# Seven half products of an expert layer in another order, and the weight sums of the first token tile made sooner

## The chip, the cores and the metric

One core of a Trainium2 chip runs the whole program. The metric is device time in microseconds (us); the core is the only one, so its time is the time. Before the change three runs gave 745.58, 746.56 and 749.73 us.

## The reference, cut to what matters

Attention with a sigmoid in place of the softmax, then a layer with three projections and a maximum, then a mixture of experts in which each token goes to one expert:

```python
for e in range(E):                       # E = 8, 1792 tokens, D = 768, F = 1024
    mask = e_idx == e
    h = np.maximum(x[mask] @ w1[e], 0.0)
    out[mask] = gate_w[mask, None] * (h @ w2[e])
```

The change lies in `h @ w2[e]`. All inputs are fp32.

## The kernel before, in words

**Token tiles.** Tokens are sorted by expert into static tiles. The first three (tile 0, 1, 2; 512, 512 and 448 tokens) take the route described here; the fourth (384 tokens, `last`) multiplies by `w2` directly, and a loop takes more tiles if there are any. Each tile has its own expert, whose weights are loaded for it: `raw[1]` (w1, three loads of 1 MB) and `raw[2]` (w2, four loads of 768 KB, one of them into the tile `rawb`).

**Precision by splitting.** Each fp32 operand is split into a rounded part and a rest (`split`, lines 183 to 189: an ACT copy, then a DVE subtraction), and each product is three matmuls: rounded by rounded, rounded by rest, rest by rounded. So every weight chunk costs ACT and DVE one instruction each (`ck_split`, line 828), and it is issued four steps ahead (`ahead`, line 1081) into a ring of six buffers.

**Steps of a tile.** n = 0 to 11: layer 1 (`mm1`, line 894), twelve chunks of 12 matmuls; four quarters q of the hidden rows, three chunks each. The results stand in PSUM banks named t, a0, a1, a0 for q = 0 to 3. n = 12 to 25: layer 2 by a scheme with seven half-size products in place of eight (Strassen's idea, in Winograd's form), two chunks of 12 matmuls (128x384) each (`mm2_prod`, line 920). The hidden half matrices are called A11, A12, A22, their sums S1 to S4, the weight quarters B11 to B22, their sums T1 to T4. The order in `PRODS` (line 825), with the bank and whether the product starts the bank or adds onto what is there:

- A11·B11 starts t; S2·T2 starts a1; A12·B21 adds onto t; S3·T3 adds onto a1; S1·T1 starts a0; A22·T4 starts t; S4·B22 adds onto a0.

I call them by these names. A product that adds onto a bank has to wait until the partial result in it was read (`read_prod`, line 933): ACT reads A11·B11 (lines 941, 942) and A12·B21 (line 944), DVE reads the others, two instructions each (line 948), scaled by the gate into four output rows `xo`. The read of product j is issued after the first chunk of product j+1.

**What else is queued on DVE in these steps.** `half_sums` (line 847) makes S1 to S4 and the splits of the A's from the banks of layer 1; four instructions of the last quarter, which read a0, are put off and issued one per step at n = 12 to 15 (`later`; lines 883 to 886, the last of them line 863 for A22). `split_sum` (line 888) splits S3, S1 and S4 in two halves, each into the buffer of a matrix that is done: S3 over A11, S1 over S2, S4 over A12. `make_sum` (line 821) makes the T's, two instructions each, in the place of B12 (T3), B11 (T1), B21 (T4) and in `tw` (T2 = T3 + B11); T1 and T4 subtract T2. `gather_T` (line 779) turns the next tile's tokens: transposes on PE after n = 19, 21 and 23, with an ACT copy and a DVE subtraction each.

**What sets the order.** PE, ACT, DVE and SP run in the order in which the program writes them; no scheduler moves anything. The main loop (line 1118) issues per step: the matmuls, `read_prod`, `split_sum` by the table `parts`, one of `later`, `gather_T`, the chunk splits four steps ahead, and `make_sum` by the table `make` (one table for tile 0, one for the others). In tile 0 the steps of layer 1 run in the order n = 0, 1, 3, 4, 6, 7, 2, 5, 8 to 11 (line 1076), and its four loads of `raw[2]` are held until the matmuls of the steps before positions 2, 3, 5 and 6 are done (line 1129).

```python
        make = [{9: "T3 0 T2 0", 10: "T3 1 T2 1", 12: "T1 0", 13: "T1 1"},
                {5: "T3 0", 6: "T2 0 T3 1", 7: "T2 1", 9: "T1 0", 10: "T1 1"}]
        parts = {2: ("S3", 0), 3: ("S3", 1), 5: ("S1", 0), 6: ("S1", 1), 9: ("S4", 0), 10: ("S4", 1)}
```

Of the kernel before, what the change touches and what calls it, by code (L numbers as in the profile page):

```python
# [16 lines left out]
ALU = mybir.AluOpType  # L17
# [11 lines left out]
def attn_moe_kernel(  # L29
# [15 lines left out]
    nc = tc.nc  # L45
# [37 lines left out]
    def cut(a, off, *shape):  # L83

        n = 1
        for s in shape:
            n *= s
        a = a[:, off:off + n]
        if len(shape) == 2:
            a = a.rearrange("p (a b) -> p a b", a=shape[0])  # L90
        elif len(shape) == 3:
            a = a.rearrange("p (a b c) -> p a b c", a=shape[0], b=shape[1])
        return a
# [89 lines left out]
    def split(dR, dL, src, alone=False):  # L183

        if alone:
            nc.vector.tensor_copy(out=r(dR), in_=src)
        else:
            nc.scalar.activation(out=r(dR), in_=src, func=ACTF.Copy)  # L188
        nc.vector.tensor_tensor(out=r(dL), in0=src, in1=dR, op=ALU.subtract)  # L189
# [183 lines left out]
    with tc.manual_schedule(engines={mybir.EngineType.PE, mybir.EngineType.Activation, mybir.EngineType.DVE, SP}):  # L373
# [84 lines left out]
        for e in range(E):  # L458
            nc.vector.scalar_tensor_tensor(out=bias_t[:, :, e], in0=midf, scalar=mb[:, 0, e:e + 1], in1=bias_t[:, :, e],
                                           op0=ALU.mult, op1=ALU.add)  # L460
# [346 lines left out]
        HC = DM // 2  # L807
# [3 lines left out]
        def quad(k, c):  # L811

            k = {"T1": "B11", "T3": "B12", "T4": "B21"}.get(k, k)
            if k == "T2":
                return tw[0][:, c]
            n = int(k[2]) - 1
            return raw[2][2 * int(k[1]) - 2 + c][:, :, HC * n:HC * (n + 1)]
# [3 lines left out]
        def make_sum(k, c):  # L821
            d, a, b = (quad(x, c) for x in (k,) + SUMS[k])
            nc.vector.tensor_tensor(out=d, in0=a, in1=b, op=ALU.add if k == "T2" else ALU.subtract)  # L823

        PRODS = (("A11", "B11", 0, True), ("S2", "T2", 1, True), ("A12", "B21", 0, False), ("S3", "T3", 1, False),
                 ("S1", "T1", 2, True), ("A22", "T4", 3, True), ("S4", "B22", 2, False))

        def ck_split(n, i=None):

# [2 lines left out]
            if n >= N1 and i is not None and i < NF:  # L832
                j, c = divmod(n - N1, 2)
                b = [cut(buf, DM * a, 2, HC) for a in range(2)]
                split(b[0], b[1], quad(PRODS[j][1], c))
                return b
# [11 lines left out]
        st = {}  # L848
# [71 lines left out]
        def mm2_prod(n, w):  # L920
            j, c = divmod(n - N1, 2)
            k, _, g, first = PRODS[j]
            if first and c == 0:
# [7 lines left out]
                                         stop=(c == 1 and f == 1 and m == 2), skip_group_check=not first)  # L931

        def read_prod(j, i, ix):
            o = st["g", PRODS[j][2]]
            for s in range(2):
                src = o[:, s, 0:HC]
                d0, d1 = xo[s], xo[2 + s]
                g0, g1 = (gcol[:, i % 2, 2 * h + s:2 * h + s + 1] for h in range(2))
                lo, hi = slice(0, HC), slice(HC, DM)
                if j == 0:  # L940
                    nc.scalar.activation(out=d0[:, hi], in_=src, func=ACTF.Copy, scale=g0)
                    nc.scalar.activation(out=d1[:, lo], in_=src, func=ACTF.Copy, scale=g1)
                elif j == 2:
                    nc.scalar.activation(out=d0[:, lo], in_=src, func=ACTF.Copy, scale=g0)
                else:
                    d, g, add = {1: (d0[:, hi], g0, d0[:, hi]), 3: (d1[:, lo], g1, d1[:, lo]), 4: (d1[:, hi], g1, d1[:, lo]),
                                 5: (d1[:, lo], g1, d1[:, lo]), 6: (d0[:, hi], g0, d0[:, hi])}[j]
                    nc.vector.scalar_tensor_tensor(out=d, in0=src, scalar=g, in1=add, op0=ALU.mult, op1=ALU.add)  # L948
                if j >= 5:
                    scatter(d1 if j == 5 else d0, ix[(2 if j == 5 else 0) + s])  # L950

# [17 lines left out]
        def scatter(d, ix):  # L969
            dm = nc.gpsimd.indirect_dma_start(out=out, out_offset=bass.IndirectOffsetOnAxis(ap=ix, axis=0),  # L970
                                              in_=d[:, 0:DM], in_offset=None, bounds_check=NT - 1, oob_is_err=False)
            if not tc.in_control_flow:
                for o_ in outs:
                    tc.declare_no_dep(dm.ins, o_, reason="each token is in one tile only")
                outs.append(dm.ins)
# [117 lines left out]
        for p in range(P0, TT):  # L1093
# [3 lines left out]
            else:  # L1097
# [12 lines left out]
        first = gather(ixs[0], (1,))  # L1110
        early = []
        steps = {N1 + 7: 0, N1 + 9: 1, N1 + 11: 2}
        make = [{9: "T3 0 T2 0", 10: "T3 1 T2 1", 12: "T1 0", 13: "T1 1"},
                {5: "T3 0", 6: "T2 0 T3 1", 7: "T2 1", 9: "T1 0", 10: "T1 1"}]
        for m in make:
            m.update({17: "T4 0", 18: "T4 1"})
        parts = {2: ("S3", 0), 3: ("S3", 1), 5: ("S1", 0), 6: ("S1", 1), 9: ("S4", 0), 10: ("S4", 1)}
        for p, (i, n) in enumerate(todo):
            last = i == NF
            nt = SH if last else MD if i == NF - 1 else GT  # L1120
# [8 lines left out]
            if i == 0 and p in (2, 3, 5, 6):  # L1129
                d = wl.popleft()()  # L1130
# [31 lines left out]
            if not last and n >= N1:  # L1162
                if n > N1 and (n - N1) % 2 == 0:
                    read_prod((n - N1) // 2 - 1, i, ixs[i])
                if n - N1 in parts:
                    split_sum(*parts[n - N1])
                if later:
                    later.popleft()()
                if n == NCW - 1:
                    read_prod(6, i, ixs[i])  # L1170
# [18 lines left out]
        d = xo[xo_n[0] % 4]  # L1189
        g = gcol[:, NF % 2, 2:3]  # L1190
# [65 lines left out]
```

## Time and profile before

| what | us |
|---|---|
| median of three runs (lowest, highest) | 746.56 (745.58, 749.73) |
| the profiled execution, its own time | 743.39 |
| its span, first to last instruction | 741.6 |
| seven products of tile 0, tile 1, tile 2, with the transposes among them | 39.2, 33.0, 33.4 |

The span is that of the one profiled execution; 1.8 us of its own time lie outside of it. A line of the profile names an engine, an operation and its source line, with the tiles it writes and reads: `oacc` are the banks of the seven products, `hacc` those of layer 1, `wo_ck` the ring of weight chunks, `hx` the split hidden matrices, `raw`, `rawb` and `tw` the weights and their sums.

### The profile page before, as it was taken

The page shows a single profiled execution, that of the slowest core. Times are in us where ns is not written, and L with a number is a line of the kernel's source. Part 1 is how long each engine was busy: PE and PEld are TensorE (multiplying, and loading weights), DVE is VectorE, ACT ScalarE, POOL GpSimd, SP SyncE. Part 2 cuts the span into 40 slices and gives each one's busy share as a digit, 9 for nine tenths or more (in the row PEclk, how much of TensorE's full clock was granted, in tenths as well). Part 3 has the DMA queues.
Part 4 walks back from the last instruction along what each step waited for, and adds up shares of the span by engine and source line. Part 5 has one row for each costly group of instructions (what it writes and reads, how often), then busy time and mean ns, then how long its engine had stood idle before and what let it go on. Part 6 is the DMA issues. An engine that isn't in the chain of part 4 may idle for free.

```text
span 741.6 us, 10670 instructions
## 1 busy us (share of the span) xinstructions
PE 726.5 (98%) x4164; PEld 615.7 (83%) x4164; DVE 486.7 (66%) x845; ACT 262.9 (35%) x410; POOL 70.4 (9%) x96
## 2 busy tenths in 40 slices
PE   9999999999999999999999999999799999999996
PEld 6455455799898989989899988988698899989996
DVE  4677784666977879684036574136983896699463
ACT  5675556001010010101025433333652373465252
POOL 3000000000000000000001007351023005000101
PEclk9999999999999999999999999999999999999999
DMA  8866670142431222300001116556063026315101
GB/s 204 210 163 162 184 203 32 44 128 85 149 108 65 85 86 63 130 0 1 1 0 45 58 51 200 175 198 269 4 219 120 1 86 230 137 40 183 57 2 62
DMA packets 42330, 78.58 MB, mean 106 GB/s; under 512 B 6201, under 2 KB 28794, under 8 KB 42276
## 3 DMA queue, kind: packets, MB, share of 16 engines
q1 hardware_dynamic: 38420, 66.10, 29.1%
q0 software_dynamic: 3776, 11.63, 4.6%
q8 instruction: 35, 0.57, 0.4%
q14 instruction: 19, 0.16, 0.1%
q10 hardware_dynamic: 80, 0.11, 0.0%
HBM read 69.79 MB, written 11.58 MB: 110 GB/s over the span
## 4 chain that ended last, share of the span: by engine, by line
PE 88%; DVE 7%; ACT 2%; issue 1%; POOL 0%; POOLq 0%; ACTq 0%; DVEq 0%
PE acc L499 35%; PE hacc L901 12%; PE X L344 8%; PE oacc L929 7%; PE s L318 7%; PE acc_b L563 5%; PE acc_a L563 4%; PE oacc L917 3%; PE acc_c L563 3%; DVE wo_ck L189 2%; PE X L352 1%; PE xT L788 1%; PE s L334 1%; DVE raw L823 1%; DVE hx L863 1%
## 5 line engine op out<-in xcount | busy, mean ns | idle before, releaser
L499 PE MATMUL acc<-xR,w_ring 128*128 128x512 f32 (+1 forms) x864 | 208.2, 362 | 0.0
L499 PEld LDWEIGHTS acc<-xR,w_ring 128*128 128x128 f32 x864 | 157.6, 188 | 17.7 <-issue 0.7
L901 PE MATMUL hacc<-xh,wo_ck 128*128 128x512 f32 (+3 forms) x600 | 121.9, 363 | 0.0
L901 PEld LDWEIGHTS hacc<-xh,wo_ck 128*128 128x128 f32 x600 | 107.2, 188 | 13.3 <-issue 0.3
L499 PE MATMUL acc<-xLa,w_ring 128*128 128x512 f32 (+1 forms) x360 | 101.3, 362 | 0.0
L929 PE MATMUL oacc<-wo_ck,hx 128*128 128x384 f32 x504 | 93.7, 341 | 7.2 <-DVE xo L948 5.4
L929 PEld LDWEIGHTS oacc<-wo_ck,hx 128*128 128x128 f32 x504 | 88.5, 191 | 9.5 <-issue 4.6
L301 ACT ACTIVATE at<-s,nlns 128x896 f32<-128x896 f32 x84 | 77.9, 1006 | 44.9 <-PE s L318 43.5
L189 DVE TENSOR_TENSOR wo_ck<-raw,wo_ck 128x512 fp32r<-128x512 f32 (+1 forms) x87 | 68.1, 805 | 24.2 <-ACT wo_ck L188 24.2
L499 PEld LDWEIGHTS acc<-xLa,w_ring 128*128 128x128 f32 x360 | 66.3, 188 | 7.1
L188 ACT ACTIVATE wo_ck<-raw 128x512 fp32r<-128x512 f32 (+1 forms) x87 | 59.6, 729 | 20.9 <-DVE raw L823 10.0
L318 PEld LDWEIGHTS s<-kq 64*128 64x128 f32 x432 | 38.1, 186 | 20.9 <-issue 15.5
L318 PE MATMUL s<-kq 64*128 64x448 f32 x432 | 51.3, 378 | 0.0
L503 ACT ACTIVATE hA<-acc 128x1024 f32<-128x1024 f32 (+1 forms) x8 | 7.4, 922 | 118.3 <-PE acc L499 118.3
L480 DVE SCALAR_TENSOR_TENSOR gk<-wof,gk 128x768 f32<-128x768 f32 x48 | 45.9, 956 | 1.4
L994 POOL MEMSET xo<- 128x544 f32 x5 | 2.6, 554 | 410.4 <-PE acc_a L563 381.8
L775 POOL DMA_INDIRECT xg<-x2d,idx x30 | 30.6, 1021 | 79.9 <-PE xT L788 50.1
L344 PE MATMUL X<-at,u 128*64 128x448 f32 x192 | 37.8, 543 | 0.0
L370 DVE CAST xR<-X 128x448 fp32r<-128x448 f32 x24 | 14.8, 619 | 32.1 <-PE X L352 32.1
L505 DVE TENSOR_TENSOR hB<-hB,acc 128x1024 f32<-128x1024 f32 (+1 forms) x8 | 8.7, 1087 | 39.5 <-PE acc L499 39.4
L188 ACT ACTIVATE w_ring<-cv 128x768 fp32r<-128x768 f32 x14 | 11.8, 842 | 54.7 <-PE acc L499 54.7
L505 DVE TENSOR_TENSOR hA<-hA,acc 128x1024 f32<-128x1024 f32 (+1 forms) x16 | 17.4, 1086 | 20.3 <-PE acc L499 19.9
(259 smaller groups left out, 885.5 us busy)
## 6 DMA issues: line engine op xcount, KB each, us to landing
stage<-in_moe_w_dram SPq DMA_DIRECT2D x18, 768.0 KB, 4.6
raw<-in_moe_w_dram SPq DMA_DIRECT2D x12, 1024.0 KB, 5.4
u<-in_qk_dram SPq DMA_DIRECT2D x46, 224.0 KB, 4.7
raw<-in_moe_w_dram SPq DMA_DIRECT2D x12, 768.0 KB, 5.6
stage<-in_moe_w_out_dram SPq DMA_DIRECT2D x6, 768.0 KB
x2d<-xo SPq DMA_DIRECT2D x28, 128.0 KB, 1.7
gk<-wgT SPq DMA_DIRECT2D x8, 384.0 KB, 5.5
rawb<-in_moe_w_dram SPq DMA_DIRECT2D x4, 768.0 KB, 5.9
```

What stands on the lines that cost most here:

```text
L188: nc.scalar.activation(out=r(dR), in_=src, func=ACTF.Copy)
L189: nc.vector.tensor_tensor(out=r(dL), in0=src, in1=dR, op=ALU.subtract)
L301: nc.scalar.activation(out=dst, in_=s[:, :, 0:S], func=ACTF.Sigmoid, scale=qscale, bias=nlns)
L318: nc.tensor.matmul(s[g][:, h, 0:S], r(kt[p, a, 0, 128 * g:128 * (g + 1)]), r(kt[p, x, 1]), start=(n == 0), stop=(n == 2))
L344: nc.tensor.matmul(X_t[u][64 * h:64 * h + 64, 0:S], vt[:, 2 * g + h], at[:, 2 * g + h], start=(g == 0), stop=False)
L480: nc.vector.scalar_tensor_tensor(out=junk, in0=wof[kb], scalar=1.0, in1=wgb[e % 2], op0=ALU.mult, op1=ALU.mult, accum_out=gw[:, kb, e:e + 1])
L499: nc.tensor.matmul(acc[:, c, 0:cw], r(m[:, a, kk, :]), r(x[kk][:, c0 + cw * c:c0 + cw * (c + 1)]), start=(kk == 0 and n == 0), stop=(kk == ...
L505: nc.vector.tensor_tensor(out=dst, in0=dst, in1=acc[:, :, 0:cw], op=ALU.max)
L563: nc.tensor.matmul(acc, r(hs[:, a, kk, :]), r(w(kk, b)), start=(kk == 0 and n == 0), stop=(kk == KB - 1 and n == 2))
L775: d = nc.gpsimd.indirect_dma_start(out=xg[s][:, XC[c][0]:XC[c][1]], out_offset=None, in_=x2d[c], in_offset=bass.IndirectOffsetOnAxis(ap=ix ...
L901: st["mm"] = nc.tensor.matmul(acc[:, f, t0:t1], r(w[a][:, k, 128 * f:128 * (f + 1)]), r(x[:, 2 * c + k, t0:t1]), start=(t0 == 0 and c == 0 ...
L929: nc.tensor.matmul(o[:, s, 0:HC], r(hz[k][:, x, 2 * c + f, 128 * s:128 * (s + 1)]), r(w[a][:, f]), start=(first and c == 0 and f == 0 and ...
```

## The change

The order of `PRODS`, of the split sums and of the reads is altered, and the sums of tile 0 get other steps. The new order is A11·B11, S2·T2, A12·B21, S1·T1, S3·T3, A22·T4, S4·B22. S1·T1 (fourth) is not read after it; with the read of S3·T3 (fifth), DVE issues four instructions: per 128 tokens one that reads a1 and one that reads a0 and adds what the first has written.

```diff
-        PRODS = (("A11", "B11", 0, True), ("S2", "T2", 1, True), ("A12", "B21", 0, False), ("S3", "T3", 1, False),
-                 ("S1", "T1", 2, True), ("A22", "T4", 3, True), ("S4", "B22", 2, False))
+        PRODS = (("A11", "B11", 0, True), ("S2", "T2", 1, True), ("A12", "B21", 0, False), ("S1", "T1", 2, True),
+                 ("S3", "T3", 1, False), ("A22", "T4", 3, True), ("S4", "B22", 2, False))
...
         def read_prod(j, i, ix):
+            if j == 3:
+                return
...
-                    d, g, add = {1: (d0[:, hi], g0, d0[:, hi]), 3: (d1[:, lo], g1, d1[:, lo]), 4: (d1[:, hi], g1, d1[:, lo]),
-                                 5: (d1[:, lo], g1, d1[:, lo]), 6: (d0[:, hi], g0, d0[:, hi])}[j]
-                    nc.vector.scalar_tensor_tensor(out=d, in0=src, scalar=g, in1=add, op0=ALU.mult, op1=ALU.add)
+                    d, g = (d0[:, hi], g0) if j in (1, 6) else (d1[:, lo], g1)
+                    nc.vector.scalar_tensor_tensor(out=d, in0=src, scalar=g, in1=d, op0=ALU.mult, op1=ALU.add)
+                    if j == 4:
+                        nc.vector.scalar_tensor_tensor(out=d1[:, hi], in0=st["g", 2][:, s, 0:HC], scalar=g, in1=d,
+                                                       op0=ALU.mult, op1=ALU.add)
...
-        make = [{9: "T3 0 T2 0", 10: "T3 1 T2 1", 12: "T1 0", 13: "T1 1"},
+        make = [{7: "T3 0 T2 0", 5: "T3 1 T2 1", 9: "T1 0", 10: "T1 1"},
                 {5: "T3 0", 6: "T2 0 T3 1", 7: "T2 1", 9: "T1 0", 10: "T1 1"}]
...
-        parts = {2: ("S3", 0), 3: ("S3", 1), 5: ("S1", 0), 6: ("S1", 1), 9: ("S4", 0), 10: ("S4", 1)}
+        parts = {3: ("S1", 0), 4: ("S1", 1), 5: ("S3", 0), 6: ("S3", 1), 8: ("S4", 0), 11: ("S4", 1)}
```

## Rows read from the trace of the kernel before

**Rows 1.** The page: busy time of each engine, share of the span, instructions.

```profile
PE 726.5 (98%) x4164; PEld 615.7 (83%) x4164; DVE 486.7 (66%) x845; ACT 262.9 (35%) x410; POOL 70.4 (9%) x96
```

**Rows 2.** Windows, tiles 0 to 2: length; PE, PEld, DVE, ACT, POOL busy; clock; DMA.

```profile
517.20:556.40 39.20, 34.45 (x193) 33.11 (x192) 33.77 (x49) 22.53 (x38) 5.72 (x6) 0.96 0.31 106
589.10:622.10 33.00, 32.14 (x194) 31.76 (x193) 29.93 (x45) 21.81 (x37) 5.01 (x6) 1.00 0.37 121
651.80:685.20 33.40, 31.82 (x189) 31.11 (x188) 30.25 (x48) 21.07 (x38) 0.97 (x1) 1.00 0.29 95
```

**Rows 3.** Timeline of PE, tile 0: start, length, line, count, idle before and its releaser.

```profile
517.18 6.43 PE L929 MATMUL oacc<-wo_ck,hx 128*128 128x384 f32 x36
524.51 0.62 PE L929 MATMUL oacc<-wo_ck,hx 128*128 128x384 f32 x2 [0.90 <-ACT wo_ck L188]
525.50 2.01 PE L929 MATMUL oacc<-wo_ck,hx 128*128 128x384 f32 x10 [0.37 <-DVE wo_ck L189]
527.86 4.46 PE L929 MATMUL oacc<-wo_ck,hx 128*128 128x384 f32 x24 [0.34 <-ACT xo L942]
535.45 5.96 PE L929 MATMUL oacc<-wo_ck,hx 128*128 128x384 f32 x24 [3.14 <-DVE xo L948]
541.25 1.04 PE L788 MATMUL xT<-ident,xg 128*128 128x128 f32 x8
```

**Rows 4.** Timeline of PE, tile 1.

```profile
589.08 12.67 PE L929 MATMUL oacc<-wo_ck,hx 128*128 128x384 f32 x72
602.61 4.40 PE L929 MATMUL oacc<-wo_ck,hx 128*128 128x384 f32 x24 [0.86 <-DVE xo L948]
606.85 1.03 PE L788 MATMUL xT<-ident,xg 128*128 128x128 f32 x8
...
617.75 4.43 PE L929 MATMUL oacc<-wo_ck,hx 128*128 128x384 f32 x24
```

**Rows 5.** Timeline of PE, tile 2.

```profile
666.28 4.40 PE L929 MATMUL oacc<-wo_ck,hx 128*128 128x384 f32 x24 [1.36 <-DVE xo L948]
```

**Rows 6.** Windows behind the wait of tile 0 (columns as in rows 2).

```profile
535.40:537.40 2.00, 1.95 (x6) 1.98 (x7) 2.00 (x3) 0.00 (x0) 0.00 (x0) 0.51 0.11 12
537.40:539.40 2.00, 2.00 (x9) 2.00 (x9) 1.71 (x3) 0.80 (x1) 0.00 (x0) 0.64 0.92 303
```

**Rows 7.** Timeline of DVE, tile 0.

```profile
504.74 0.69 DVE L877 SCALAR_TENSOR_TENSOR sums<-hacc,sums 128x512 f32<-128x512 f32 x1 [6.54 <-ACT hx L876]
...
509.26 0.68 DVE L866 SCALAR_TENSOR_TENSOR sum<-hacc,sums 128x512 f32<-128x512 f32 x1
...
514.02 1.81 DVE L189 TENSOR_TENSOR wo_ck<-raw,wo_ck 128x768 fp32r<-128x768 f32 x2
515.75 0.95 DVE L823 TENSOR_TENSOR raw<-raw 128x768 f32<-128x768 f32 x1
516.74 0.96 DVE L823 TENSOR_TENSOR tw<-raw 128x768 f32<-128x768 f32 x1
```

**Rows 8.** Timeline of DVE, tile 1.

```profile
590.23 0.68 DVE L866 SCALAR_TENSOR_TENSOR sum<-hacc,sums 128x512 f32<-128x512 f32 x1
...
593.31 0.96 DVE L189 TENSOR_TENSOR wo_ck<-tw,wo_ck 128x768 fp32r<-128x768 f32 x1 [1.01 <-ACT wo_ck L188]
...
597.18 0.69 DVE L189 TENSOR_TENSOR hx<-sums,hx 128x512 fp32r<-128x512 f32 x1
...
599.86 0.68 DVE L863 SCALAR_TENSOR_TENSOR hx<-hacc,hx 128x512 fp32r<-128x512 f32 x1
...
615.28 1.14 DVE L948 SCALAR_TENSOR_TENSOR xo<-oacc,gcol,xo 128x384 f32<-128x384 f32 x2
```

**Rows 9.** Timeline of ACT, tile 1.

```profile
596.03 0.61 ACT L942 ACTIVATE xo<-oacc,gcol 128x384 f32<-128x384 f32 x1
```

**Rows 10.** Timeline of SP, tile 0: issue of the last weight load of layer 2.

```profile
500.89 0.37 SPq L767 DMA_DIRECT2D rawb<-in_moe_w_dram  x1
```

**Rows 11.** The line of the weight loads: issue to landing, all 28 loads.

```profile
DMA to landing us min/median/max: 4.3/5.5/7.4
```

## Prediction

> **What bounds the kernel now.** I read the page first: PE is busy for 98% of the span [rows 1], so only its idle stretches, and stretches at a lower clock, can be won. The windows over the three product stages [rows 2] say where these are: PE is idle for 39.20 - 34.45 = 4.75 us in tile 0, 0.9 us in tile 1 and 1.6 us in tile 2, and the stage of tile 0 is 6 us longer than the others with the same matmuls. The timeline of PE names what ended each wait. In tile 0, S2·T2 waits 0.90 and 0.37 us for the split of its second weight chunk, A12·B21 waits 0.34 us for ACT's read of bank t, and S3·T3 waits 3.14 us for DVE's read of a1 (line 948) [rows 3]. The same wait for line 948 costs 0.86 us in tile 1 [rows 4] and 1.36 us in tile 2 [rows 5]. It is a wait for DVE's queue, not for data: S2·T2 was done a whole product earlier, and DVE works through 29.9 of tile 1's 33.0 us [rows 2]. Behind the 3.14 us the granted clock was 0.51 and then 0.64 for 4 us [rows 6], that is 1.2 GHz in part, and S3·T3 took from 535.45 to 541.25 = 5.80 us to the transposes behind it [rows 3], where tile 1 needs 606.85 - 602.61 = 4.24 [rows 4]: 1.56 us more. So the read of a1 costs 3.14 + 1.56 + 0.86 + 1.36 = 6.92 us in all.
>
> **The change part by part.** PE's work is the same (seven products at 24 matmuls, as many transposes), ACT's and POOL's instructions are the same in number, and DVE's too (ten reads of products per tile; the ten become two, four, two and two). No load is added or moved in SP's queue. Everything is a matter of order in DVE's queue.
>
> *1. The sums of tile 0, T3 and T2.* One DVE sum takes 0.87 us from start to start; the dependent T2 starts 516.74 - 515.75 = 0.99 us after its T3 [rows 7]. The pair of the first half moves in front of the DVE instruction at 504.74, before which DVE sat idle for 6.54 us [rows 7]: it is hidden there, and if that cover were gone it would cost 1.9 us. The pair of the second half comes after n = 5, which is straight ahead of line 866 at 509.26 [rows 7]: nothing hides it there, so line 866 and the queue behind it move back by 2 x 0.87 = 1.74 us. The first two chunk splits of layer 2, now at 514.02 [rows 7], then run at 515.76 to 517.50; the first is through at 516.6, before A11·B11 starts at 517.18 [rows 3], and the second is wanted half a product (2.1 us) later. Costs nothing.
>
> *2. T1 of tile 0 one per step, as in tile 1.* Behind the splits come T1, a split, T1 (3 x 0.87 = 2.61 us), so that line 866 of the last quarter starts at 517.50 + 2.61 = 520.1. From there the queue is that of tile 1, where line 866 starts at 590.23 [rows 8]; the shift is 70.1 us. The split of T2's second half ends in tile 1 at 593.31 + 0.96 = 594.27 [rows 8], so in tile 0 at 524.15, and PE goes on with it just after. A product takes 4.2 us (72 matmuls in 12.67 [rows 4], 0.175 each), so PE comes to that half at 517.2 + 1.5 x 4.2 = 523.5; two of its matmuls need only ACT's part, the other ten last 1.75: S2·T2 ends at 526.0, with some 0.4 us of wait left. ACT's last read of A11·B11 ends in tile 1 at 596.03 + 0.61 = 596.64 [rows 9], in tile 0 at 526.5, and A12·B21 starts at 526.65 in place of 527.86 [rows 3]: 1.2 us won. Two waits (0.4 and 0.65) stay, from the 1.74 us of step 1.
>
> *3. S1·T1 fourth.* It waits for no read of a product. What it needs last on DVE is line 863, which frees a0 from layer 1. In tile 1 that starts at 599.86 [rows 8]; ahead of it in the queue two splits of S3 (the first at 597.18 [rows 8], 0.60 us each) go and one of S1 comes, so it starts at 599.26 and ends at 599.94. A12·B21 ends 72 matmuls after 589.08, at 601.75 [rows 4]: DVE is 1.8 us early, and the 0.86 us go. Taken 70.1 us earlier it ends in tile 0 at 529.8, against PE's 526.65 + 4.2 = 530.8: 1.0 us early. So S1·T1 starts there at 530.8 in place of S3·T3 at 535.45, and without a long wait the clock does not fall: at the transposes behind the fourth product PE stands at 530.8 + 4.25 = 535.05 in place of 541.25, 6.2 us won (the 1.2 us of step 2 within it). Tile 1 wins 0.86 and tile 2 1.36: together 8.4 us. The ACT half of S1's first split overwrites S2, and waits until the first half of S2·T2 is done (595.4 in tile 1, a product and a half after 589.08 [rows 4]); ACT comes to it after its reads, which end at 596.64 [rows 9], so this new wait is covered by 1.2 us or more.
>
> *4. S3·T3 fifth.* It adds onto a1 a product later than before, so the read of a1 has 4.25 us more. The order T3, S3, T4 in DVE's queue behind it moves by at most four instructions of 0.6 to 0.9 us, and each is wanted over 2 us after it is made. Nothing.
>
> *5. Four reads ahead of the last product.* S4·B22 adds onto a0, which is now read with S3·T3's bank: four DVE instructions where there were two. In tile 1 the two start at 615.28 and take 1.14 us [rows 8]. The second of each new pair adds what the first wrote; the row nearest to that is the pair of T3 and T2 above, 0.12 us more than without [rows 7]. So the four end at 615.28 + 2 x 1.14 + 2 x 0.12 = 617.8, and S4·B22 now starts at 617.75 [rows 4]: the margin is nil. The bounds are 0 (DVE has two reads fewer ahead of them and comes to them sooner) and 1.1 us per tile (the two additional reads in full). I take 0.5 us for the three tiles together.
>
> **The sum**: 8.4 - 0.5 = 7.9 us, or 735.5 for the profiled execution of 743.39 us. That execution stands 3.2 us below the median; I take the gain off the median, 746.56 - 7.9 = 738.7.
>
> **Rivals.** *A. The wait moves to a0.* S1·T1 has its bank to itself only between line 863 and the four reads. If both margins (1.0 us in tile 0 and 1.8 in tile 1; nil at the other end) are smaller than worked out, the wait is there instead: 1.1 us per tile for the reads, 3.3 us, and the gain is 5.1: 741.5. For it: the margin of step 5 is next to nothing. Against it: two reads fewer stand ahead of the four, so DVE comes to them sooner.
>
> *B. DVE is the bound.* It is busy for 30 of the 33 us of a stage [rows 2], and no DVE work goes away. If waits of 0.9 and 1.4 us only move to where DVE is late next, tiles 1 and 2 win nothing, and tile 0 wins what leaves its stage, four sums at 0.87 = 3.5 us: 743.1. Against it: PE's own 7 x 4.24 + 3 x 0.81 = 32.1 us is above DVE's 30 (a product and its transposes take (617.75 - 602.61) / 3 = 5.05 us [rows 4]).
>
> *C. The lower clock is no part of the runs that set the median.* The trace is one execution, with one such stretch [rows 6]. Without those 1.56 us the gain is 6.3: 740.3. The Trainium skill (TensorE: Matmul & The Clock Gate, section What's actually happening) says that the point at which the clock changes differs from run to run of one kernel; by that the same wait may cost the clock in one run and not in another. No run here shows it yet.
>
> *D. Slower: the second pair of sums waits for its load.* It now stands at the head of DVE's queue from 509.3 on, with all of layer 2's splits behind it, and needs `rawb`, issued at 500.89 [rows 10]; now it stands behind the T2 of 516.74 [rows 7]. A landing 8.4 us after the issue would be met without loss, each us beyond that is one us of PE, and from 8.4 + 7.9 = 16.3 us on the change loses; 22 us is 13.6 us too late, a loss of 5.7: 752.3. Against it: no weight load took more than 7.4 us [rows 11].
>
> *E. The reorder does nothing.* That would need S1·T1 to wait until DVE's read of a1 is done all the same. The code gives no reason for it, as the bank is another; it has no chance of its own.
>
> **How the numbers follow.** The forecast has 0.60, C 0.10, A 0.13, B 0.11, D 0.04; 0.02 is for what I don't see. A measurement of this kernel can tell about 0.5%, 3.7 us, from no change: faster means below 742.8. The forecast, C and most of A lie there, and a third of B: 0.82. Same 0.13, slower 0.05. The range: below, the two waits of step 2 (1.05 us) and those of step 5 (0.5 us) might go too, 737.1, and one more us stands for the scatter of the median, whose runs lie from 745.58 up; above, A and C together (5.1 - 1.56 = 3.5 us of gain) give 743.1, and I stop at 743.0, which leaves out half of B and all of D. From 736.1 to 743.0.
>
> **What would show it.** Right: no wait of `oacc` for line 948 ahead of the fourth product; the fourth product follows the third at once in all three tiles; the clock 1.00 through tile 0's stage, and the stage 33 to 34 us long, with waits under 1 us for a chunk's split and for line 942; T2's last sum done at about 511. Wrong: a wait of 0.5 us or more ahead of S4·B22 for line 948 or for the new read (A), waits ahead of S1·T1 for line 863 or ahead of S3·T3 for a split of S3 or a chunk (B), a DVE instruction of line 823 that waits for a DMA near 509 (D). If the stage of tile 0 keeps its 39 us though no wait for line 948 is left, the reason given here is wrong.

## The result, and the profile after

| | before | after |
|---|---|---|
| median of four runs each, us (lowest, highest) | 747.56 (745.58, 749.73) | 739.04 (738.53, 739.59) |
| ratio after to before, 95% interval | | 0.9886 (0.9854 to 0.9917) |
| the profiled execution: its own time, span | 743.39, 741.6 | 739.59, 737.8 |
| stages of tile 0, 1, 2 | 39.2, 32.9, 33.2 | 33.6, 31.9, 32.1 |

The kernel is 8.5 us faster (6.2 to 10.9 us by the ends of the interval, times 747.56). The forecast was 738.7 us. A stage is counted here, and in all that follows, from the first matmul of the seven products to 4.25 us (24 matmuls) behind the start of the last product. The three stages together are 5.6 + 1.0 + 1.1 = 7.7 us shorter.

First the timeline of PE in the changed kernel, tile 0, tile 1 and tile 2 (it answers to rows 3 to 5):

```profile
521.18 6.78 PE L929 MATMUL oacc<-wo_ck,hx 128*128 128x384 f32 x38
528.32 2.01 PE L929 MATMUL oacc<-wo_ck,hx 128*128 128x384 f32 x10 [0.37 <-DVE wo_ck L189]
530.67 8.60 PE L929 MATMUL oacc<-wo_ck,hx 128*128 128x384 f32 x48 [0.34 <-ACT xo L944]
539.11 1.03 PE L788 MATMUL xT<-ident,xg 128*128 128x128 f32 x8
...
549.21 1.04 PE L788 MATMUL xT<-ident,xg 128*128 128x128 f32 x8
550.50 4.40 PE L929 MATMUL oacc<-wo_ck,hx 128*128 128x384 f32 x24 [0.25 <-issue]
...
587.42 16.83 PE L929 MATMUL oacc<-wo_ck,hx 128*128 128x384 f32 x96
...
615.10 4.42 PE L929 MATMUL oacc<-wo_ck,hx 128*128 128x384 f32 x24
...
657.83 8.62 PE L929 MATMUL oacc<-wo_ck,hx 128*128 128x384 f32 x48 [0.22 <-ACT xo L944]
...
676.99 4.43 PE L929 MATMUL oacc<-wo_ck,hx 128*128 128x384 f32 x24 [0.23 <-DVE xo L951]
```

A12·B21 and S1·T1 now run as one group of 48 matmuls, in tile 1 the first four products as one of 96: nothing waits ahead of the fourth product any more. What is left are the two short waits of tile 0 (for a chunk's split and for ACT's read), one like the second in tile 2, and one ahead of the last product.

The windows over the stages (columns as in rows 2) show PE idle for 1.0, 0.0 and 0.5 us, where it was 4.75, 0.9 and 1.6 [rows 2], and the clock at 1.00 in tile 0 too:

```profile
521.20:554.80 33.60, 32.64 (x194) 31.68 (x193) 31.45 (x47) 21.81 (x37) 5.31 (x5) 1.00 0.36 124
587.40:619.40 32.00, 32.00 (x194) 31.80 (x193) 29.71 (x45) 21.81 (x37) 4.48 (x5) 1.00 0.37 124
649.10:681.30 32.20, 31.75 (x188) 31.11 (x188) 30.11 (x47) 21.06 (x37) 0.85 (x1) 1.00 0.29 98
```

The timeline of DVE in tile 0 (to rows 7 and 8): the first pair of sums in the old gap, the second pair straight ahead of line 866, then line 863 for A22, the read of a1 and the four reads:

```profile
503.74 0.95 DVE L823 TENSOR_TENSOR raw<-raw 128x768 f32<-128x768 f32 x1
504.73 0.96 DVE L823 TENSOR_TENSOR tw<-raw 128x768 f32<-128x768 f32 x1
...
513.26 0.95 DVE L823 TENSOR_TENSOR raw<-rawb,raw 128x768 f32<-128x768 f32 x1
514.25 0.96 DVE L823 TENSOR_TENSOR tw<-raw 128x768 f32<-128x768 f32 x1
515.12 0.68 DVE L866 SCALAR_TENSOR_TENSOR sum<-hacc,sums 128x512 f32<-128x512 f32 x1
...
533.18 0.68 DVE L863 SCALAR_TENSOR_TENSOR hx<-hacc,hx 128x512 fp32r<-128x512 f32 x1
533.78 0.95 DVE L189 TENSOR_TENSOR wo_ck<-raw,wo_ck 128x768 fp32r<-128x768 f32 x1
534.65 1.14 DVE L949 SCALAR_TENSOR_TENSOR xo<-oacc,gcol,xo 128x384 f32<-128x384 f32 x2
...
547.91 0.61 DVE L949 SCALAR_TENSOR_TENSOR xo<-oacc,gcol,xo 128x384 f32<-128x384 f32 x1
548.55 0.62 DVE L951 SCALAR_TENSOR_TENSOR xo<-oacc,gcol,xo 128x384 f32<-128x384 f32 x1
549.09 0.61 DVE L949 SCALAR_TENSOR_TENSOR xo<-oacc,gcol,xo 128x384 f32<-128x384 f32 x1
549.73 0.62 DVE L951 SCALAR_TENSOR_TENSOR xo<-oacc,gcol,xo 128x384 f32<-128x384 f32 x1
```

For comparison, two rows of the kernel before: the read of a1, and the two reads of S1·T1 that stood where the four stand now:

```profile
534.17 1.13 DVE L948 SCALAR_TENSOR_TENSOR xo<-oacc,gcol,xo 128x384 f32<-128x384 f32 x2
...
549.65 1.14 DVE L948 SCALAR_TENSOR_TENSOR xo<-oacc,gcol,xo 128x384 f32<-128x384 f32 x2
```

From the start of the third product the read of a1 comes 4.0 us later (534.65 - 530.67), where it was 6.3 (534.17 - 527.86 [rows 3]). It still ends about 0.9 us behind the end of that product (535.79, against 530.67 + 4.25 = 534.92); but S3·T3, which needs it, begins only at 539.90.

One thing does not fit at first sight: the span is only 741.6 - 737.8 = 3.8 us shorter, though the stages are 7.7 us shorter. The changed kernel's profile comes to tile 0 at 521.18, the old one at 517.18 [rows 3]: 4.0 us are lost ahead of all that was changed. The experiments had to say whether the change does that.

### The profile page after: what moved, and what is told of

Its sections match the earlier page's. It is cut to its first block, busy times and chain, and to the rows that moved or that the text cites. A ratio compares the mean times of both kernels' runs of the same rounds, so it can differ in the third digit from the quotient of the medians.

```text
span 737.8 us, 10663 instructions
## 1 busy us (share of the span) xinstructions
PE 725.3 (98%) x4164; PEld 614.4 (83%) x4164; DVE 486.9 (66%) x845; ACT 262.8 (36%) x410; POOL 74.5 (10%) x96
## 4 chain that ended last, share of the span: by engine, by line
PE 88%; DVE 6%; ACT 2%; issue 1%; DMA 1%; POOL 0%; SPq 0%; POOLq 0%; ACTq 0%; DVEq 0%
PE acc L499 35%; PE hacc L901 13%; PE X L344 8%; PE oacc L929 7%; PE s L318 7%; PE acc_b L563 5%; PE acc_a L563 4%; PE oacc L917 3%; DVE wo_ck L189 2%; PE acc_c L563 2%; PE X L352 1%; PE s L334 1%; PE xT L788 1%; DVE raw L823 1%; ACT wo_ck L188 1%
## 5 line engine op out<-in xcount | busy, mean ns | idle before, releaser
L929 PE MATMUL oacc<-wo_ck,hx 128*128 128x384 f32 x504 | 91.1, 337 | 1.4 <-ACT xo L944 0.6
L775 POOL DMA_INDIRECT xg<-x2d,idx x30 | 35.1, 1170 | 80.7 <-PE xT L788 44.5
L344 PE MATMUL X<-at,u 128*64 128x448 f32 x192 | 37.8, 543 | 0.0
```

The costliest lines, as they stand in the source:

```text
L344: nc.tensor.matmul(X_t[u][64 * h:64 * h + 64, 0:S], vt[:, 2 * g + h], at[:, 2 * g + h], start=(g == 0), stop=False)
L775: d = nc.gpsimd.indirect_dma_start(out=xg[s][:, XC[c][0]:XC[c][1]], out_offset=None, in_=x2d[c], in_offset=bass.IndirectOffsetOnAxis(ap=ix ...
L929: nc.tensor.matmul(o[:, s, 0:HC], r(hz[k][:, x, 2 * c + f, 128 * s:128 * (s + 1)]), r(w[a][:, f]), start=(first and c == 0 and f == 0 and ...
```

## The experiments

Lead-in, stages and time in us; the lead-in is the time of the first matmul of tile 0's products in the profiled execution. The time is the median, with the number of runs; times from different chips can't be compared. On which chips the first two rows ran is not known.

| run | chip | lead-in | tile 0 | tile 1 | tile 2 | time (runs) |
|---|---|---|---|---|---|---|
| before | not known | 517.2 | 39.2 | 32.9 | 33.2 | 747.56 (4) |
| changed | not known | 521.2 | 33.6 | 31.9 | 32.1 | 739.04 (4) |
| before again | 15 | 517.8 | 39.3 | 32.9 | 33.2 | 744.12 (1), 743.83 (8) |
| order only | 15 | 517.6 | 36.5 | 31.9 | 32.1 | 738.73 (4) |
| sums only | 15 | 516.9 | 34.8 | 32.9 | 33.2 | 739.05 (5) |
| reads early | 15 | 517.5 | 33.1 | 31.8 | 31.7 | 735.51 (1) |
| wait short | 11 | 521.3 | 37.4 | 31.9 | 32.1 | 744.01 (1) |
| wait long | 11 | 520.3 | 40.4 | 31.9 | 32.1 | 745.98 (1) |
| loads early | 11 | 527.0 | 31.9 | 31.9 | 32.1 | 744.09 (1) |
| load late | 11 | 520.2 | 35.0 | 31.9 | 32.1 | 740.11 (1) |
| changed again | 7 | 520.8 | 33.6 | 31.9 | 32.1 | 738.85 (4) |
| reads early, timed | 7 | 521.2 | 33.1 | 31.8 | 31.7 | 738.80 (4) |
| reads early, sums at n = 2 | 7 | 521.6 | 31.8 | 31.8 | 31.6 | 737.86 (4) |

Beside these the kernel before took 747.71 us on chip 11 (one run) and 746.59 on chip 7 (seven runs), without a profile.

**The kernel before, once more.** No edit.

> The kernel before, profiled once more. Theory (the waits come from the order of DVE's queue, so they repeat): product stages of 39.2, 33.0 and 33.2 us again within 0.1, a wait of 3.1 us for line 948 in tile 0 and a granted clock near 0.5 behind it. Rival C (the lower clock is an affair of single runs): the clock stays at 1.00 behind that wait, and the stage of tile 0 is 37.6 us. The 4 us by which the changed kernel's profile came later to tile 0 lie outside of the stages; if they are scatter of single runs, this profile too reaches tile 0 at another time than 517.18.

Measured: the stages within 0.05 us, 3.17 us of wait for line 948, and 5.82 us for S3·T3. The windows behind the wait (columns as in rows 2):

```profile
536.00:538.00 2.00, 1.94 (x9) 1.97 (x10) 2.00 (x3) 0.00 (x0) 0.00 (x0) 0.75 0.08 9
538.00:540.00 2.00, 2.00 (x8) 2.00 (x7) 1.72 (x3) 0.79 (x1) 0.00 (x0) 0.50 0.89 281
540.00:542.00 2.00, 2.00 (x13) 1.97 (x12) 1.83 (x2) 0.06 (x1) 0.00 (x0) 0.90 0.83 272
```

In the first profile the third of these windows was:

```profile
539.40:541.40 2.00, 2.00 (x14) 1.97 (x13) 1.83 (x2) 0.05 (x1) 0.00 (x0) 1.00 0.80 266
```

The clock falls again, a little later (0.75, 0.50, 0.90 where it was 0.51, 0.64 [rows 6] and 1.00), and costs the same. Rival C falls for this kernel as far as two executions go.

**The order alone.**

```diff
-        make = [{7: "T3 0 T2 0", 5: "T3 1 T2 1", 9: "T1 0", 10: "T1 1"},
+        make = [{9: "T3 0 T2 0", 10: "T3 1 T2 1", 12: "T1 0", 13: "T1 1"},
```

> The new order of products, reads and split sums, with the weight sums of tile 0 at their old steps. Theory: tile 0 starts its fourth product when line 863 is through, about 0.8 us after the third product's end (in the old trace line 863 would end at 532.8, the third product at 532.0), with no fall of the clock; stage of tile 0 35.4 us (39.2 before, 33.6 changed), tiles 1 and 2 32.0 and 32.1 as in the changed kernel. Gain 5.9 us, 741.7. Rival (without the sums moved, DVE is as late for line 863 as it was for line 948): tile 0 keeps a wait of about 3 us and the clock falls, stage 38 us or more, gain 2 to 3 us, about 745.

Measured: 738.73 us beside 743.83 for the kernel before on that chip, ratio 0.9934 (0.9909 to 0.9960), that is 4.9 us; the stages say 2.7 + 1.0 + 1.1 = 4.8. Tile 0 by PE's timeline:

```profile
528.27 4.46 PE L929 MATMUL oacc<-wo_ck,hx 128*128 128x384 f32 x24 [0.33 <-ACT xo L944]
533.35 4.40 PE L929 MATMUL oacc<-wo_ck,hx 128*128 128x384 f32 x24 [0.62 <-ACT hx L188]
...
547.70 1.03 PE L788 MATMUL xT<-ident,xg 128*128 128x128 f32 x8
549.84 4.42 PE L929 MATMUL oacc<-wo_ck,hx 128*128 128x384 f32 x24 [1.11 <-DVE xo L951]
```

and the timeline of DVE, line 863 for A22:

```profile
532.52 0.69 DVE L863 SCALAR_TENSOR_TENSOR hx<-hacc,hx 128x512 fp32r<-128x512 f32 x1
```

The fourth product waits 0.62 us in place of 3.14, near the 0.8 expected, and the clock stays at 1.00. Line 863 ends at 533.21, just ahead of the start; the profile names an ACT split that ends within 0.05 us of it, so this run by itself does not tell which of the two the product waited for. What I had not put into the expectation is the wait of 1.11 us ahead of the last product: DVE is still behind there, and the four reads are late by what rival A said, in full. So the stage is 36.5, not 35.4 us. (The median of 738.73 is no match for the 739.04 of the whole change: it comes from a chip on which the kernel before is faster too.)

**The sums alone.** The same line of `make` the other way round: the kernel before with the new steps for tile 0.

> The old order of products, with the weight sums of tile 0 at their new steps. Theory: line 948 is through 15.3 us after the stage's start in place of 18.1, S3 times T3 waits 1.6 us and the clock does not fall; stage of tile 0 34.8 us, tiles 1 and 2 33.0 and 33.2 as before; gain 4.4 us, 743.1. With the run of the order alone the two gains add up to 10.3, more than the 7.7 of both, as each alone spares the same 1.56 us of lower clock and part of the same wait. Rival (the sums are worth only the 1.2 us at A12 times B21 of step 2, and the wait stays above 3 us): stage 38 us, gain 1.2, 746.4.

Measured: 739.05 us, ratio 0.9946 (0.9923 to 0.9969), 4.0 us; the stage of tile 0 is 34.8 us as expected, the other two as before.

```profile
532.33 4.40 PE L929 MATMUL oacc<-wo_ck,hx 128*128 128x384 f32 x24 [1.50 <-DVE xo L948]
```

The wait for the read of a1 is still there, and halved; the clock stays at 1.00 behind it. In tile 0 the two parts alone win 2.7 and 4.4 us, 7.1 together, and both at once 5.6. The difference of 1.5 us is near what the lower clock cost, which each spares by itself: without those 1.56 us it is 1.1 + 2.8 = 3.9 us for the two alone and 4.1 for both. That the rest fits so well is in part chance. Counted from the stage's start, the fourth product starts at 18.27 us before, 15.76 with the order, 15.43 with the sums and 13.68 with both: the parts share 0.76 us of the wait as well. About as much comes back ahead of the last product, where the order alone loses 1.35 us (549.84 - 547.70 = 2.14 from the transposes, 0.79 before) and both together only 0.50.

**The four reads one step sooner.**

```diff
-                if n > N1 and (n - N1) % 2 == 0:
+                if n > N1 and (n - N1) % 2 == 0 and n != N1 + 10:
                     read_prod((n - N1) // 2 - 1, i, ixs[i])
+                if n == N1 + 9:
+                    read_prod(4, i, ixs[i])
```

> The changed kernel with the four reads ahead of the last product issued one step sooner, straight behind the fifth product's second chunk, ahead of that step's split sum, gather and chunk split. Theory (the last product waits for these reads: 0.5, 0.1 and 0.5 us): stages 33.1, 31.8 and 31.7 us, 1.1 us shorter together. Rival (DVE is simply full, so the gathers' subtraction and the chunk split come as much later as the reads come sooner): the wait ahead of S4 times B22 goes over to a chunk's split or to the transposes, stages unchanged within 0.2 us or longer.

Measured: 33.10, 31.81 and 31.66 us, the expected numbers. DVE now takes the four reads ahead of the gather's subtraction (line 797) and a chunk split, neither of which PE was waiting for:

```profile
542.21 0.61 DVE L949 SCALAR_TENSOR_TENSOR xo<-oacc,gcol,xo 128x384 f32<-128x384 f32 x1
542.86 0.62 DVE L951 SCALAR_TENSOR_TENSOR xo<-oacc,gcol,xo 128x384 f32<-128x384 f32 x1
543.39 0.61 DVE L949 SCALAR_TENSOR_TENSOR xo<-oacc,gcol,xo 128x384 f32<-128x384 f32 x1
544.03 0.62 DVE L951 SCALAR_TENSOR_TENSOR xo<-oacc,gcol,xo 128x384 f32<-128x384 f32 x1
544.57 1.28 DVE L797 TENSOR_TENSOR xh<-xT,xh 128x512 fp32r<-128x512 f32 x2
```

The first and the last product of tile 0 on PE:

```profile
517.53 6.78 PE L929 MATMUL oacc<-wo_ck,hx 128*128 128x384 f32 x38
...
546.38 4.42 PE L929 MATMUL oacc<-wo_ck,hx 128*128 128x384 f32 x24
```

So the last product did wait for these reads in the changed kernel, 1.05 us over the three tiles, also in tile 0, where the profile had put the wait down to issue. This run contains the whole change and comes to tile 0 at 517.53, like the kernel before.

**A short and a long wait ahead of the fourth product.** In tile 0 alone, six or ten additions on a tile that nothing else uses, ahead of line 863:

```diff
+                if i == 0 and n == N1 + 3:
+                    for _ in range(6):
+                        nc.vector.tensor_tensor(out=dum, in0=dum, in1=dum, op=ALU.add)
                 if later:
                     later.popleft()()
```

> The changed kernel with six idle DVE additions of 128x384 (0.53 to 0.62 us each, 3.2 to 3.7 us) ahead of line 863 in tile 0 alone. Theory: line 863 has a margin of 0.9 us, so S1 times T1 waits 2.3 to 2.8 us, under the 3.14 us that cost the clock before; the clock stays at 1.00 and the stage is longer by that wait alone, 35.9 to 36.4 us, unless the reads ahead of the last product, whose margin is nil, are late too by what DVE has not caught up. Rival (any wait of 2 us or more costs the clock): granted clock near 0.5 behind it and 1.5 us more, about 37.8.

> The same with ten additions (5.3 to 6.2 us). Theory: S1 times T1 waits 4.4 to 5.3 us, the clock falls behind the wait as it did before, and the stage is longer by the wait and some 1.6 us: 39.6 to 40.5 us. Rival (the fall of the clock in the kernel before had another cause than the wait, as the transfer that starts there): the clock stays at 1.00 and the stage is 38 to 38.9 us.

Measured with the short wait: PE's timeline, and the windows over the wait and behind it (columns as in rows 2):

```profile
537.52 5.99 PE L931 MATMUL oacc<-wo_ck,hx 128*128 128x384 f32 x24 [2.32 <-DVE hx L865]
543.35 1.04 PE L790 MATMUL xT<-ident,xg 128*128 128x128 f32 x8
```

```profile
535.20:537.50 2.30, 0.00 (x1) 0.01 (x1) 2.23 (x5) 1.57 (x3) 0.00 (x0) 1.00 0.00 0
537.50:539.50 2.00, 1.98 (x8) 2.00 (x9) 2.00 (x4) 0.00 (x0) 0.00 (x0) 0.66 0.00 0
539.50:541.50 2.00, 2.00 (x8) 2.00 (x7) 2.00 (x4) 0.00 (x0) 0.00 (x0) 0.50 0.00 0
```

With the long wait, PE's timeline:

```profile
538.97 6.67 PE L931 MATMUL oacc<-wo_ck,hx 128*128 128x384 f32 x24 [4.72 <-DVE hx L865]
545.47 1.04 PE L790 MATMUL xT<-ident,xg 128*128 128x128 f32 x8
```

(Line numbers are two higher, as the tile `dum` took two lines.) The long wait came out within what was expected, 40.4 us, though the lower clock cost more than the 1.6 us reckoned with: S1·T1 took 545.47 - 538.97 = 6.50 us in place of 4.25. With the short one I was wrong: a wait of 2.32 us also brought the clock to 0.50, S1·T1 took 543.35 - 537.52 = 5.83 us in place of 4.25, and the stage is 37.4 us, near the rival's 37.8. No byte was moved by DMA in these three windows, so transfers like those that began behind the old wait [rows 6] are not needed for the fall. Behind the 1.50 us of the sums alone the clock had stayed at 1.00. Where between these it turns was not tried.

**The w2 loads and all four sums early.**

```diff
-        make = [{7: "T3 0 T2 0", 5: "T3 1 T2 1", 9: "T1 0", 10: "T1 1"},
+        make = [{7: "T3 0 T2 0 T3 1 T2 1", 9: "T1 0", 10: "T1 1"},
...
-            if i == 0 and p in (2, 3, 5, 6):
+            if i == 0 and p in (2, 3, 4, 5):
```

> The changed kernel with the four w2 loads of tile 0 at positions 2, 3, 4, 5 and all four sums T3, T2 of tile 0 at step n = 7, in the DVE gap ahead of line 877. Theory: line 866 of the third quarter no longer stands behind the second pair of sums, so DVE is 1.86 us earlier in tile 0's stage; the waits of 0.4 us (S2 times T2) and 0.34 to 0.65 us (A12 times B21) go, and the stage of tile 0 is 32.6 to 32.9 us in place of 33.56. Rival D (the load of rawb lands too late for the gap, and DVE stands behind it): a wait for the DMA at line 823 of some us; as DVE has 3 us of room there, a stage above 33.6 only if the landing is over 9 us after the issue.

Measured: the profiled execution took 744.09 us. The stage itself is 31.9 us, without a wait. But DVE stood at the head of its queue for two loads, and layer 1 behind it:

```profile
507.40 0.96 DVE L823 TENSOR_TENSOR raw<-raw 128x768 f32<-128x768 f32 x1 [2.12 <-DMA raw<-in_moe_w_dram]
508.39 0.96 DVE L823 TENSOR_TENSOR tw<-raw 128x768 f32<-128x768 f32 x1
512.08 0.96 DVE L823 TENSOR_TENSOR raw<-rawb,raw 128x768 f32<-128x768 f32 x1 [2.73 <-DMA rawb<-in_moe_w_dram]
```

```profile
517.17 10.03 PE L901 MATMUL hacc<-xh,wo_ck 128*128 128x512 f32 x36 [2.84 <-DVE hx L863]
```

PE waited 2.84 us in layer 1 for a bank that DVE had not read, the clock fell behind that (0.50 in the window 519 to 521), and from the last transposes to the first product it took 27.4 us in place of 22.8. The expectation had looked at the stage alone. `rawb` was issued at 503.48 and released its sum at 512.08: 8.6 us, longer than any of the 28 loads of before [rows 11]. That is rival D's mechanism, with a load that was issued sooner and came no sooner: counted from the last transposes, it was issued at 3.8 us and released its sum at 12.4; in the run with the sums at n = 2 below, issued at 6.5, it was there by 12.2. Why it took longer is not shown: the DMA engines were busy for over 0.9 of the time in both.

**The load of `rawb` held back.** Its issue is moved from ahead of the matmuls at position 6 to behind those at position 7.

> The changed kernel with the load of rawb held until the matmuls of step n = 5 are done, some 5.2 us later than now. Theory (rival D's mechanism is real, but its point lies 8.4 us after the issue): the load lands 4.3 to 7.4 us after its issue, so T3 waits 1 to 4 us for the DMA at the head of DVE's queue; of that, 0.5 us is margin at the stage's start and the rest is a us of PE for each us: stage of tile 0 plus its lead-in longer by 0.5 to 3.5 us. Rival (DVE makes it good, as there are later gaps): line 823 waits and the PE comes to tile 1 no later.

Measured, in DVE's timeline:

```profile
513.70 0.96 DVE L823 TENSOR_TENSOR raw<-rawb,raw 128x768 f32<-128x768 f32 x1 [1.31 <-DMA rawb<-in_moe_w_dram]
```

The load is issued at 509.38, T3 waits for it until 513.70, 1.31 us at the head of the queue, and tile 0's end comes 1.4 us later (stage 35.0, and from the last transposes to the stage 22.8 us as without the edit). So what DVE loses here PE loses, one for one; neither the 0.5 us of margin nor a later gap made it good.

**The changed kernel again, the early reads timed, and the second pair of sums at n = 2.** Three kernels on one chip, beside the kernel before (746.59 us there). The third has the edit of the early reads and

```diff
-        make = [{7: "T3 0 T2 0", 5: "T3 1 T2 1", 9: "T1 0", 10: "T1 1"},
+        make = [{7: "T3 0 T2 0", 2: "T3 1 T2 1", 9: "T1 0", 10: "T1 1"},
```

> The changed kernel once more, timed beside the kernel before and the two below on one chip. Theory: the product stages repeat within 0.1 us (33.6, 31.9, 32.1), so it is 7.7 us faster than the kernel before on the same chip; where the profile shows no wait of PE for the gathered tokens (xT for xg) ahead of tile 0, tile 0 begins near 517 and the span is near 734, where it shows one, near 521 and 738. That lead-in belongs to the chip and not to the change. Rival (the change itself delays the gathers and costs some 3.5 us ahead of tile 0): tile 0 begins at 520 or later whatever the chip.

> The four reads one step sooner, as in the run of the reads alone, now timed. Theory: 1.1 us under the changed kernel on the same chip (stages 33.1, 31.8, 31.7). Rival: what the stages win is lost in scatter or in the next tile, no difference.

> The same, and the second pair of tile 0's sums (T3 1, T2 1) issued after step n = 2 in place of n = 5, one step sooner, with the loads where they are. Theory: the pair then fills DVE's gap of 0.83 us ahead of the second line 877, line 866 of the third quarter comes 0.8 us sooner, and the waits of S2 times T2 (0.4) and A12 times B21 (0.34) shrink: stage of tile 0 32.3 to 32.6 us, another 0.5 to 0.8 us. Rival D (rawb has not landed by then; in the run with the loads early it took 8.6 us, here the sum stands 5.7 us after the issue): DVE waits for the DMA up to 2.9 us with the layer 1 reads behind it, PE comes to tile 0 later, and the kernel is up to 2 us slower than with the reads alone.

Measured: 738.85 us (ratio to the kernel before 0.9904, interval 0.9870 to 0.9937), 738.80 (0.9887, 0.9867 to 0.9908) and 737.86 (0.9879, 0.9857 to 0.9902). The changed kernel is 746.59 - 738.85 = 7.7 us faster than the kernel before on this chip, as the stages say. The stages of the first two repeat to 0.02 us, but the 1.1 us of the early reads can't be told from no change by these times: the intervals overlap almost wholly. The third has the shortest time of all, and its stage of 31.8 us is free of waits; again part of that is paid ahead of the stage, where the first chunk of layer 1's last quarter now waits for a0, which DVE reads 0.9 us later than in the changed kernel (first T3 1 on DVE, which does not wait for its load, then PE):

```profile
510.02 0.95 DVE L823 TENSOR_TENSOR raw<-rawb,raw 128x768 f32<-128x768 f32 x1
```

```profile
513.31 8.45 PE L901 MATMUL hacc<-xh,wo_ck 128*128 128x512 f32 x36 [0.81 <-DVE hx L863]
521.60 16.83 PE L929 MATMUL oacc<-wo_ck,hx 128*128 128x384 f32 x96
```

From the last transposes ahead of tile 0 to its end the three take 56.4, 55.9 and 55.6 us, so the sums at n = 2 are worth 0.35 us, not the 0.5 to 0.8 expected. It beats the changed kernel in the profile by 1.05 + 0.35 us, and by 1.0 us in the medians, which the intervals don't resolve.

The lead-in: all three come to tile 0 at 521 on this chip. The kernel with the early reads, which contains the whole change, comes at 521.2 here and came at 517.5 on the chip of its first run, where the kernel before came at 517.8. So it goes with the chip and not with the change: the rival falls. (Each chip was used in one session only, so what about the chip or the session does it is open.) But my sign for it was too narrow: the changed kernel came at 520.8 with no wait for the gathered tokens, only with waits that the profile puts down to issue. On the chip with the early lead-in the kernel before takes 743.83 us (eight runs), in its other timed runs 746.6 to 747.7.

## Why the prediction was right

**What bounds it**: right. The waits for the read of a1 were waits for DVE's queue. The sums alone, which take DVE work out of tile 0's stage, halve the wait there; the order alone, which takes the read off PE's next product, removes it in all three tiles.

**Steps 1 and 2**, tile 0's sums: right. Line 866 of the last quarter stands 3.0 us behind the stage's start (524.22), worked out as 2.9; the two waits that were to stay are there with 0.37 and 0.34 us by PE's rows. They were worked out as 0.4 and 0.65 us, so the second is 0.3 us shorter. The sums alone gave the stage of 34.8 us that the same reckoning gives.

**Step 3**, S1·T1 fourth: right. Line 863 starts 12.0 us after the stage's start, as worked out (529.2 - 517.2), the margin was there in all three tiles, and the clock did not fall. The three stages were to win 7.9 us net of step 5, and won 7.7. That this is so near is in part luck, as two errors offset each other: with the early reads, which take away the cost of step 5, the stages win 6.1 + 1.1 + 1.6 = 8.8 us where 8.4 were reckoned, and step 5 cost some 0.5 us more than reckoned. The first error has a source in the rows: the length of a row of matmuls reaches past the start of what follows (602.61 + 4.40 = 607.01, the transposes start at 606.85 [rows 4]), so the idle time behind it is shown too short. The wait of 0.86 us in tile 1 cost 1.11, the 1.36 us in tile 2 cost 1.57.

**Step 5**, the four reads: the right place and half the size. I took 0.5 us for three tiles, and the early reads show 0.47 + 0.12 + 0.46 = 1.05 us. The dependent pair did cost 0.64 us from start to start in place of 0.53 (rows of the four reads), 0.11 us each, near the 0.12 by the row of T3 and T2. The reckoning hoped that DVE would come to the reads sooner, with two reads fewer ahead of them. What it missed is that PE comes to the last product sooner by as much or more: in tile 0, counted from the stage's start, DVE begins the reads 5.7 us sooner (26.73 in place of 32.47), and PE comes to the last product, where nothing holds it, 6.1 us sooner (28.85 in place of 34.96).

**The clock**: the size of 1.56 us was right. The thought behind it, "without a long wait the clock does not fall", left open how long; I took it for some 3 us, and 2.32 us were long enough. The longest wait left in the stage was 0.5 us, so nothing hung on it. On rival C: behind the same wait the granted clock changes at another point in each of the two executions of the kernel before, and the cost was 1.56 and 1.58 us, so it made no difference to the time. The Trainium skill (TensorE: Matmul & The Clock Gate, section What's actually happening) says of the clock's rise behind the start of a kernel that its point varies from run to run. The two traces agree, for the fall and the rise behind this wait.

**Rivals.** A is real, at a third of its price: with the order alone its wait is 1.11 us in tile 0, and in the changed kernel 0.47, just under the 0.5 that was named as its sign, and 1.05 us over the three tiles where A had 3.3. B falls: tile 1 won 1.0 us where 0.86 were counted, and tile 2 1.1, or 1.6 with the early reads, where 1.36 were counted; with the early reads PE runs through tile 1 without a wait. D didn't come true, with less room than I thought: the bound of 7.4 us [rows 11] was no bound, as one load took 8.6 us in another run, and the second pair of sums stands 8.4 us behind the issue of its load.

**The median.** Taking the gain off the median, and not off the profiled execution, came out right, but no reason was given for it, so that was luck. By their lead-ins (517.2 and 521.2) the profile of before comes from a chip like 15 and the one after from a chip like 7 and 11; its time of 743.39 us, below all four runs of its own median and like those on chip 15, says the same, but on which chips they ran is not known. The 0.3 us between forecast and measurement are less than the 1.0 us by which a fourth run moved the median of before.

## What to carry to other kernels

When an engine in the middle is full for most of a stage, ask of each wait in it whether the consumer can take something else first: here the product with a bank of its own filled the gap while DVE caught up, and the order alone won 4.8 of the 7.7 us by the stages. The gains of two edits that spare the same long wait can't be added, since the lower clock behind it is saved once, and shared parts of the wait too. And an instruction that waits for a load at the head of an in-order queue costs what everything behind it is worth: pulling it into an earlier gap won 1.7 us in the stage and lost 4.6 us ahead of it.

## What was not expected of the hardware

A wait of PE of 2.32 us, in a stretch that was busy before, was followed by a granted clock of 0.50, like the waits of 3.14 and 4.72 us and the 2.84 us in layer 1; 1.50 and 1.11 us were not. The same kernel (the one with the early reads) reached tile 0 3.7 us later on one chip than on another, with the same instructions; the other profiles, but for the one with the loads early, fall into the same two groups by chip. In the late ones waits for gathered tokens or for issue stand in the 60 us ahead of tile 0. So two profiles from two chips can't be subtracted over their whole spans. A load of 768 KB that was issued earlier released its sum 8.6 us after its issue, where held back it did so after 4.3.
